# Tap products in an idle half of the result tile, a reciprocal-root chain one group later, and the last group's PSUM bank sets exchanged

## The chip, the core and the metric

The kernel runs on one core of a Trainium2 chip. The metric is the device time of one execution in microseconds (us). The engines are PE (TensorE, matrix products; PEld is its loading of the stationary operand), DVE (VectorE), ACT (ScalarE), POOL (GpSimd) and SP (SyncE); each runs its own instructions in order and waits on semaphores for the others. DMAs are issued from SP and from POOL.

## What is computed

The input x has the shape (8, 4224, 192). The first block is a causal depthwise convolution over the sequence with 7 taps; the 192 channels are in 8 heads of 24, and each head has one softmaxed set of taps. The second block normalizes each row of the result y (mean and variance over 192 channels), multiplies by a 192x768 matrix, applies relu, multiplies by a 768x192 matrix, and adds y.

```
w = softmax(weight, axis=-1)
out = np.einsum('hk,bskhg->bshg', w, x_unf)      # x_unf: 7 shifted copies of x
mu, var = mean(x), mean((x - mu)**2)             # x is out of the first block
xn = (x - mu) / np.sqrt(var + 1e-06) * g_ln
return x + np.maximum(xn @ w_ch1, 0.0) @ w_ch2
```

## The kernel before, in words

**Groups.** The rows are cut into 18 groups, 128 partitions with up to 16 rows (J) each. Group 0 has 6 rows per partition, group 1 has 8 (what is left over from all batches), groups 2 to 16 have 16, and group 17, the last, has 10. The centring and the gain are folded into the first matrix, and the reciprocal root of the variance (rstd) is applied to a row's result at the very end, since relu commutes with a positive factor. Groups 0 and 1 are multiplied plainly (`up`, `down`). From group 2 on, the two products are done by a Strassen-like scheme with seven products of quarter matrices in place of eight (`up_mixed` and `up_last`, then `down_fast`): sums of quarters of the weights and of y are formed ahead, and partial results are added from PSUM or by DMA.

**Order.** The schedule is by hand: each engine gets its instructions in the order in which the Python code emits them. While PE works on group g, ACT, DVE and POOL prepare group g+1. The convolution of a group is made of three pieces: ACT writes the first tap's product into y (`first_tap`, L366, instructions of L375), then the second tap's into a tile tb (`second_tap`, L385, instructions of L383), which is added to y by four accumulating DMAs that POOL issues (`add_in_parts`, L402, instructions of L406); DVE adds the other taps (`conv`, L414). For group 2 there is a `third_tap` as well: it writes into a tile third, is added to tb[2] by four DMAs, and DVE adds tb[2] to y with one large addition (L1051).

**Buffers.** tb has one buffer (pool tag "tb"), and so has "cs", from which third[2] comes. A second user of a tag waits until the first user's last reader is done. The result of the first product is held in `room`, one tile of 6·16·128 floats per partition (tag "ht"). Groups 0 and 1 use only its lower half or less; during the start the upper half holds constants and the raw weights. From group 2 on the whole tile is used. The results of groups 0 and 1 share one output tile ot (L931).

**PSUM.** There are eight banks. `take_set` (L123) hands out four at a time, the lower or the upper four; `take_bank` (L118) one at a time, in turn. The up stage of a group from 2 on takes two sets, called X and Y; then `down_fast` takes six banks, beginning with the one that stood first in the up stage. Its bank for column block c and product kind i is banks[2c + i] (L849 to L853): kind 0 uses the first, third and fifth, and kind 1 the others.

**The up stage of groups 2 to 16** (`up_mixed`, L601). There are two passes, `one` over a third of a quarter's columns and `two` over the rest, each of seven products that alternate between X and Y. Results that must be added to a quarter that is already in `room` go in one of two ways (`close`, L636): DVE adds them from PSUM (L640), or ACT copies them out (L634) and POOL issues an accumulating DMA (`add_by_dma`, L599). In pass `one` there are three such DMAs, whose sources lie in places of `room` that pass `two` writes later; so ACT's eviction of `two.c22` (L694) waits until the third has landed. Two calls of next(pending) stand between them: `pending` is the generator `root` (L447), 19 small POOL operations that compute rstd by Newton steps, nine before its first yield and ten after it. `act_scales` (L654) makes ACT scale two rows of the group before, one of them ahead of the eviction of c21 (L691), the second further on.

**The down stage** (`down_fast`, L839) has seven products on PE and sums on DVE (L899); ACT evicts (L862). Between the products it works through a list `work`, which up_mixed returns: relus, the scaling of the remaining rows of the group before (`scale`, L936, instructions of L938), the DMAs that add them to the output in DRAM (`add_to_out`, L940, issued by POOL at L949), and the first and second taps of group g+2.

**Around groups 0 to 2.** After down(0), the main loop calls `next(root(0, True))` (L1046), which emits all 19 POOL operations for groups 0 and 1 at once. In `down(1)` ACT evicts each row from PSUM with the scale applied (L812), and group 0's six rows are scaled and added to the output at its first step; parts of second_tap(3) stand between the evictions (L817). In group 1's step the main loop also emits DVE's convolution of group 2, its sums (L590 to L594, with POOL's L595 and L596), and the sums of weight quarters on POOL (L571). Group 1's output is added in group 2's work list (L721).

**The last group** (`up_last`, L726) has one pass with X and Y. Its last product goes into X, from where ACT evicts it with relu (L776). Then DVE lowers quarters (L834), and `down_fast` starts with the product of c11 (the quarter a[:, 0, 0]).

Of the kernel before, what the change touches and what calls it, by code (L numbers as in the profile page):

```python
# [7 lines left out]
F32 = mybir.dt.float32  # L8
# [8 lines left out]
def kernel(  # L17
# [29 lines left out]
    nc = tc.nc  # L47
# [337 lines left out]
    def second_tap(g, heads=(0, H)):  # L385

        if heads[0] == 0:
            tb[g] = bpool.tile([P, J, D], F32, tag="tb", name=f"tb{g}")
        tap_products(g, tb[g], 1, heads)
        if g > 2 and heads[1] == H:  # L390
            add_in_parts(g, y[g], tb[g])
# [3 lines left out]
    def third_tap(g, heads):  # L395
        if heads[0] == 0:
            third[g] = cpool.tile([P, J, D], F32, tag="cs", name=f"third{g}")
        tap_products(g, third[g], 2, heads)
        if heads[1] == H:
            add_in_parts(g, tb[g], third[g])  # L400
# [45 lines left out]

    def root(g, whole=False):  # L447
        both = [k for k in (g, g + 1) if k < NG and chain_of(k) == g]
# [25 lines left out]
        for step in range(3):  # L474
            nc.gpsimd.tensor_tensor(d, r, r, op=ALU.mult)  # L475
            nc.gpsimd.tensor_tensor(d, d, v, op=ALU.mult)  # L476
            if step == 0 and not whole:
                yield
            affine(d, d, -0.5, 1.5)
            nc.gpsimd.tensor_tensor(r, r, d, op=ALU.mult)  # L480
# [120 lines left out]
    def up_mixed(g, ahead, pending):  # L601
# [7 lines left out]
        s1, s2, s3, s4 = ysums[g]  # L609
        done = groups[g - 1][2] if fast[g - 1] else 0  # L610

# [42 lines left out]
        def act_scales(j1, j2):  # L654
            if done:
                scale(g - 1, j1, j2)

# [54 lines left out]
        def scale_one(j):  # L712
            scale(g - 1, j, j + 1)
            if j == 7:
                add_to_out(g - 1, 0, 8)
            elif j == done - 1:
                add_to_out(g - 1, 8, done)

        work = [lambda: one.relu(one.c22)]
        if g == 2:  # L720
            work += [lambda: add_to_out(1, 0, groups[1][2])] + [lambda: None] * 5  # L721
        work += [lambda j=j: scale_one(j) for j in range(2, done)]
# [3 lines left out]
    def up_last(g, ahead, pending):  # L726
# [22 lines left out]

        X, Y = take_set(), take_set()  # L750
        product(X, a11, b11, True, False)
# [46 lines left out]
    def down(g):  # L798
# [3 lines left out]
        for j in range(0, groups[g][2], 2):  # L802
            bank = take_bank()[:, 0 : 2 * D].rearrange("p (j d) -> p j d", d=D)
            for i in range(2):
                down_row(bank[:, i], lambda f: ht[g][:, f, j + i].rearrange("p q t -> p (q t)"))
            if g == 0:
                nc.scalar.copy(ot[:, j : j + 2, :], bank)
                if j:
                    third_tap(2, (0, 4) if j == 2 else (4, H))
                continue  # L810
            for i in range(j, j + 2):
                nc.scalar.mul(ot[:, i, :], bank[:, i - j], rstd[g][:, i : i + 1])  # L812
            if j == 0:
                scale(0, 0, groups[0][2])
                add_to_out(0, 0, groups[0][2])
            elif j < 6:
                second_tap(3, heads=(2, 5) if j == 2 else (5, H))  # L817

# [20 lines left out]
    def down_fast(g, work):  # L839
# [8 lines left out]
        parts = [free[:, 0:CH], free[:, CH : 2 * CH]]  # L848
        banks = [take_bank() for c in range(CH) for i in range(2)]  # L849

        def product(bank, left, right, to, first, behind=0):
# [83 lines left out]

    def scale(g, j1, j2):  # L936
        for j in range(j1, j2):
            nc.scalar.mul(ots[g][:, j, :], ots[g][:, j, :], rstd[g][:, j : j + 1])  # L938
# [77 lines left out]
    for g in range(NG):  # L1016
# [9 lines left out]
        if g == 0:  # L1026
# [18 lines left out]
            down(g)  # L1045
            next(root(0, True))  # L1046
            continue
        if g == 1:
# [13 lines left out]
            sums_of_quarters(w2sums[:, 1], b22, w2sums[:, 0])  # L1062
            sums_of_quarters(w2sums[:, 3], b21, w2sums[:, 1])
            continue
        if g + 2 < NG:
# [44 lines left out]
```

## Time and profile before

| | |
|---|---|
| runs shown | 961.76, 961.92, 963.83 us |
| median | 961.92 us |
| the profiled execution | 965.22 us |
| its span in the profile | 963.4 us |
| mean granted TensorE clock | 0.995 |
| POOL: DMAs that add to the output, L949 | 70 issues, 0.97 us each |
| ACT: scaling of rows, L938 | 230 instructions, 0.47 us each |
| median time from issue to landing: adds into room from room (512 KB) | 5.2 us |
| the same: adds of tap products to y (384 KB) | 8.9 us |

The span is that of the instructions that the profiler saw; the execution's own time lies 1.8 us above it. A profiled execution can differ from the runs without a profile; here it is 3.3 us above their median.

How to read it: a line of a timeline gives the start and the length in us, the engine, the line of the kernel, the operation, the tile written and the tile read, and how often; brackets at the end hold the idle time ahead of it and what ended that. A list of waits gives who waited for whom, with the total, the number of waits and the longest. A table of windows gives, for each stretch, its length, then the busy time of PE, PEld, DVE, ACT and POOL with their instructions, then the granted clock of TensorE, the share of the DMA engines and the rate in GB/s. "issue" as the releaser means that the profile shows nothing that was waited for; the landing of a DMA can be behind it.

### The profile page before, as it was taken

To read this page: it belongs to the slowest core of one execution; us is meant where nothing else is said; L and a number is where in the kernel's file an instruction comes from. 1 tells how busy PE (TensorE), PEld (TensorE's weight loads), DVE (VectorE), ACT (ScalarE), POOL (GpSimd) and SP (SyncE) were. 2 spreads that over 40 slices of the span, in tenths; PEclk is the share of its full clock that TensorE was granted. 3 is DMA by queue.
4 is the path that set the end of the run, shared out by engine and by line. 5 is a ranking of instruction groups with operands and counts; after the bars stand their busy time and mean duration, and the time that the engine had idled before them with its cause. 6 is when DMAs were issued, how large, how long until landed. Compare 5 with 4: busy or idle time off the path is not lost. (4 is left out here: it accounts for less than half of the span.)

```text
span 963.4 us, 38488 instructions
## 1 busy us (share of the span) xinstructions
PE 945.3 (98%) x17106; PEld 751.3 (78%) x17106; DVE 892.4 (93%) x1479; ACT 715.6 (74%) x1271; POOL 344.0 (36%) x463
## 2 busy tenths in 40 slices
PE   9999699999999999999999999999999999999998
PEld 7999558677785989778796967768596877869587
DVE  8995989999999999999999999999999999997885
ACT  6957566968788795968779696877879596767552
POOL 2077316141544218141452316241351425332140
PEclk9999999999999999999999999999999999999999
DMA  9387985897979787897978988797988888776641
GB/s 204 120 188 184 224 228 103 215 205 141 257 143 252 148 238 154 193 227 130 276 133 239 176 205 184 141 267 146 249 152 232 169 176 205 131 171 123 100 66 47
DMA packets 38347, 171.94 MB, mean 178 GB/s; under 512 B 4517, under 2 KB 5798, under 8 KB 32039
## 3 DMA queue, kind: packets, MB, share of 16 engines
q0 software_dynamic: 31488, 106.87, 60.3%
q1 hardware_dynamic: 6688, 62.61, 18.0%
q8 instruction: 134, 2.20, 0.9%
q14 instruction: 31, 0.25, 0.1%
q10 hardware_dynamic: 6, 0.00, 0.0%
HBM read 38.92 MB, written 50.92 MB: 93 GB/s over the span
## 5 line engine op out<-in xcount | busy, mean ns | idle before, releaser
L414 DVE SCALAR_TENSOR_TENSOR y<-xg,taps,y 128x384 f32<-128x384 f32 (+3 forms) x710 | 358.8, 580 | 13.9 <-issue 13.3
L856 PE MATMUL ps<-room,w2sums 128*32 128x256 f32 (+1 forms) x4464 | 243.1, 376 | 0.0
L634 ACT COPY room<-ps 128x512 f32<-128x512 f32 (+1 forms) x225 | 180.6, 845 | 65.6 <-PE ps L520 61.5
L520 PE MATMUL ps<-yt,w 32*128 32x256 f32 (+3 forms) x4092 | 226.3, 365 | 1.0 <-ACT ot L812 0.5
L520 PEld LDWEIGHTS ps<-yt,w 32*128 32x128 f32 x4092 | 203.2, 185 | 19.0 <-issue 6.8
L856 PEld LDWEIGHTS ps<-room,w2sums 128*32 128x32 f32 x4464 | 148.7, 110 | 88.7
L856 PE MATMUL ps<-room,w 128*32 128x256 f32 (+1 forms) x3456 | 194.6, 379 | 7.6 <-DVE room L640 5.7
L856 PEld LDWEIGHTS ps<-room,w 128*32 128x32 f32 x3456 | 115.2, 112 | 78.6 <-DVE room L640 10.8
L899 DVE TENSOR_TENSOR room<-room 128x1024 f32<-128x1024 f32 x135 | 154.6, 1218 | 19.1 <-PE ps L856 11.1
L520 PE MATMUL ps<-ysums,w1sums 32*128 32x256 f32 (+1 forms) x2304 | 132.2, 371 | 0.0
L520 PEld LDWEIGHTS ps<-ysums,w1sums 32*128 32x128 f32 x2304 | 121.3, 185 | 5.3 <-issue 0.2
L949 POOL DMA_DIRECT2D out_dram<-ot x70 | 60.4, 967 | 173.3 <-ACT ot L938 161.2
L862 ACT COPY cs<-ps 128x256 f32<-128x256 f32 (+1 forms) x192 | 70.9, 369 | 56.8 <-PE ps L856 56.4
L647 ACT ACTIVATE room<-room 128x1024 f32<-128x1024 f32 x90 | 94.8, 1063 | 4.1 <-DMA room<-parts_cs 4.1
L938 ACT ACTIVATE ot<-ot,r 128x192 f32<-128x192 f32 x230 | 97.2, 468 | 0.0
L406 POOL DMA_DIRECT2D y<-tb x59 | 52.9, 1426 | 116.1 <-ACT room L862 95.6
L520 PE MATMUL ps<-yt,w1sums 32*128 32x256 f32 (+1 forms) x1152 | 71.9, 372 | 2.8 <-ACT room L634 2.8
L375 ACT ACTIVATE y<-xg,taps 128x384 f32<-128x384 f32 (+3 forms) x141 | 72.9, 605 | 1.5 <-DMA xg<-in_x_dram 0.8
L383 ACT ACTIVATE tb<-xg,taps 128x384 f32<-128x384 f32 (+1 forms) x128 | 69.8, 625 | 5.5 <-DVE w1sums L568 5.5
L520 PE MATMUL ps<-ysums,w 32*128 32x256 f32 (+1 forms) x1152 | 71.2, 369 | 0.0
L445 DVE BATCH_NORM_STATS2 st<-y 128x6 f32<-128x192 f32 x264 | 70.2, 344 | 0.0
L862 ACT COPY room<-ps 128x256 f32<-128x256 f32 (+1 forms) x96 | 35.5, 371 | 44.0 <-PE ps L856 43.4
(125 smaller groups left out, 962.4 us busy)
## 6 DMA issues: line engine op xcount, KB each, us to landing
xg<-in_x_dram SPq DMA_DIRECT2D x14, 2112.0 KB, 15.9
out_dram<-ot POOLq DMA_DIRECT2D x61, 384.0 KB, 9.5
room<-room POOLq DMA_DIRECT2D x45, 512.0 KB, 5.2
y<-tb POOLq DMA_DIRECT2D x58, 384.0 KB, 8.9
out_dram<-y SPq DMA_DIRECT2D x14, 1536.0 KB, 9.5
room<-parts_cs POOLq DMA_DIRECT2D x30, 512.0 KB, 6.9
room<-parts_tb POOLq DMA_DIRECT2D x15, 1024.0 KB, 7.6
xg<-in_x_dram SPq DMA_DIRECT2D x1, 1848.0 KB
```

What stands on the lines that cost most here:

```text
L375: nc.scalar.mul(y[g][:, 0:n, cs], xg[g][:, 0:n, cs], taps[:, h, 0:1])
L383: nc.scalar.mul(dst[:, 0:n, cs], xg[g][:, k : k + n, cs], taps[:, h, k : k + 1])
L414: nc.vector.scalar_tensor_tensor(out=y[g][:, 0:n, cs], in0=t[:, k : k + n, cs], scalar=taps[:, h, k : k + 1], in1=y[g][:, 0:n, cs], op0=AL ...
L445: nc.vector.bn_stats(out=sums[g][:, j, :], in_=y[g][:, j, :])
L520: nc.tensor.matmul(banks[:, q, i * w + j1 * t : i * w + j2 * t], right[rows, c, P * i : P * i + P], left[rows, j1:j2, c, :], start=start, ...
L634: nc.scalar.activation(to, of, AF.Relu) if relu else nc.scalar.copy(to, of)
L647: nc.scalar.activation(c, c, AF.Relu)
L856: nc.tensor.matmul(dst[C * q : C * q + C, 0:w], right[:, f, C * c : C * c + C], left[:, f, q], start=(first and f == PAIR), stop=(f == PAI ...
L862: nc.scalar.copy(to[:, c], dst[:, 0:w].rearrange("p (j t) -> p j t", t=t))
L899: nc.vector.tensor_tensor(dst[:, f], left[:, f], right_of[:, f], op=op)
L938: nc.scalar.mul(ots[g][:, j, :], ots[g][:, j, :], rstd[g][:, j : j + 1])
L949: nc.gpsimd.dma_start(out=rows[:, d0:d1], in_=src[:, d0:d1], accum_op=ALU.add)
```

## The change

- tb[2] and third[2] are no longer tiles of their own: they are the two quarters of the upper half of `room`. The other groups' tb keep their tile.
- `root(0)` is no longer emitted after down(0). It becomes `pending` at the end of group 1's step, so that its two pieces are emitted in group 2's up stage, at the two calls of next(pending).
- `down(1)` evicts as `down(0)` does, two rows with one plain copy. The rows of groups 0 and 1, 14 together, are scaled in group 2 (two in the up stage, twelve in the work list of its down stage), and both groups are added to the output from that list. The second taps of group 3 are spread over the first three evictions of down(1), two or so heads after each.
- In the last group, X and Y are exchanged: X is the upper set. `down_fast` reorders its six banks there, so that kind 0 uses the first three and kind 1 the other three.

```
     def second_tap(g, heads=(0, H)):
-        if heads[0] == 0:
+        if heads[0] == 0 and g == 2:
+            tb[g] = room[:, NF * J * Q :][:, 0 : J * D].rearrange("p (j d) -> p j d", d=D)
+        elif heads[0] == 0:
             tb[g] = bpool.tile([P, J, D], F32, tag="tb", name=f"tb{g}")
...
     def third_tap(g, heads):
         if heads[0] == 0:
-            third[g] = cpool.tile([P, J, D], F32, tag="cs", name=f"third{g}")
+            third[g] = room[:, NF * J * Q + J * D :].rearrange("p (j d) -> p j d", d=D)
...
-    def root(g, whole=False):
+    def root(g):
...
-            if step == 0 and not whole:
+            if step == 0:
                 yield
...
     def up_mixed(g, ahead, pending):
-        done = groups[g - 1][2] if fast[g - 1] else 0
+        before = g - 1 if fast[g - 1] else 0
+        done = sum(groups[k][2] for k in range(before, g))
...
         def act_scales(j1, j2):
-            if done:
-                scale(g - 1, j1, j2)
+            scale(before, j1, j2)
...
         def scale_one(j):
-            scale(g - 1, j, j + 1)
-            if j == 7:
-                add_to_out(g - 1, 0, 8)
-            elif j == done - 1:
-                add_to_out(g - 1, 8, done)
+            scale(before, j, j + 1)
+            for k in range(before, g):
+                n = groups[k][2]
+                first, mid = (0 if k == before else groups[before][2]), min(8, n)
+                if j == first + mid - 1:
+                    add_to_out(k, 0, mid)
+                elif j == first + n - 1:
+                    add_to_out(k, mid, n)
...
-        if g == 2:
-            work += [lambda: add_to_out(1, 0, groups[1][2])] + [lambda: None] * 5
...
     def up_last(g, ahead, pending):
-        X, Y = take_set(), take_set()
+        Y, X = take_set(), take_set()
...
     def down(g):
-            if g == 0:
-                nc.scalar.copy(ot[:, j : j + 2, :], bank)
-                if j:
-                    third_tap(2, (0, 4) if j == 2 else (4, H))
-                continue
-            for i in range(j, j + 2):
-                nc.scalar.mul(ot[:, i, :], bank[:, i - j], rstd[g][:, i : i + 1])
-            if j == 0:
-                scale(0, 0, groups[0][2])
-                add_to_out(0, 0, groups[0][2])
-            elif j < 6:
-                second_tap(3, heads=(2, 5) if j == 2 else (5, H))
+            nc.scalar.copy(ot[:, j : j + 2, :], bank)
+            if g == 0 and j:
+                third_tap(2, (0, 4) if j == 2 else (4, H))
+            elif g == 1 and j < 6:
+                second_tap(3, heads=[(2, 4), (4, 6), (6, H)][j // 2])
...
     def down_fast(g, work):
         banks = [take_bank() for c in range(CH) for i in range(2)]
+        if g + 1 == NG:
+            banks = [banks[CH * i + c] for c in range(CH) for i in range(2)]
...
             down(g)
-            next(root(0, True))
             continue
...
             sums_of_quarters(w2sums[:, 3], b21, w2sums[:, 1])
+            pending = root(0)
             continue
```

## The prediction

> **What bounds the kernel.** I read the busy shares first. PE (TensorE) is busy 98% of the span and is full in nearly every slice; the fifth slice is the exception, the only place after the start where it drops visibly.
>
> ```profile
> PE 945.3 (98%) x17106; PEld 751.3 (78%) x17106; DVE 892.4 (93%) x1479; ACT 715.6 (74%) x1271; POOL 344.0 (36%) x463
> ...
> PE   9999699999999999999999999999999999999998
> ```
>
> So an edit pays only where PE waits, or where its clock falls. PE's own waits, second view, are few:
>
> ```profile
> PE ps L856 <- DVE room L640: 5.7, 2, 5.3
> PE ps L520 <- ACT room L634: 2.8, 3, 2.2
> ...
> PE ps L856 <- ACT room L776: 1.9, 1, 1.9
> PE ps L520 <- ACT ot L812: 0.5, 1, 0.5
> ```
>
> The timeline places them: 0.54 us at 82.9, 2.17 at 104.8 and 5.33 at 112.4, all in group 2 (the first full group), and 1.87 at 937.2 in the last group. Third view, PE in order of time (start, length, count, and in brackets the idle time before):
>
> ```profile
> 106.92 2.87 PE L520 MATMUL ps<-yt,w1sums 32*128 32x256 f32 x48 [2.17 <-ACT room L634]
> 109.62 2.77 PE L520 MATMUL ps<-yt,w 32*128 32x256 f32 x48
> 117.71 7.02 PE L856 MATMUL ps<-room,w 128*32 128x256 f32 x72 [5.33 <-DVE room L640]
> 124.56 7.94 PE L856 MATMUL ps<-room,w2sums 128*32 128x256 f32 x144
> 132.33 4.06 PE L856 MATMUL ps<-room,w 128*32 128x256 f32 x72
> ```
>
> 72 equal matmuls take 7.02 us after the long wait and 4.06 later: 2.96 lost to the clock. The windows (PE's granted clock is the figure ahead of the last two) agree, and show the same at the end:
>
> ```profile
> 116.00:118.00 2.00, 0.29 (x4) 0.20 (x8) 1.90 (x2) 0.00 (x0) 0.00 (x0) 0.72 1.17 151
> 118.00:120.00 2.00, 2.00 (x24) 0.94 (x20) 2.00 (x2) 0.00 (x0) 0.00 (x0) 0.50 0.89 96
> ...
> 941.00:943.00 2.00, 2.00 (x48) 1.98 (x44) 2.00 (x4) 0.40 (x2) 0.00 (x0) 0.52 0.04 8
> ```
>
> At the end, 72 narrow matmuls at 939.08 take 3.73 us, against 2.15 for the same form at 946.67: 1.58 lost.
>
> **Why PE waits in group 2.** DVE reaches the sum of L640 late because it sat idle for 12.30 us, waiting for the four DMAs that add group 3's tap products to y (L406). POOL issued those only behind other things:
>
> ```profile
> 80.19 2.86 POOL L595 TENSOR_TENSOR ysums<-yt 128x768 f32<-128x768 f32 x1 [2.82 <-DVE ysums L594]
> 83.00 1.80 POOL L949 DMA_DIRECT2D out_dram<-ot  x2
> 84.17 4.17 POOL L406 DMA_DIRECT2D y<-tb  x4
> 86.35 3.82 POOL L596 TENSOR_TENSOR yt<-yt,ysums 128x768 f32<-128x768 f32 x1
> ...
> 93.36 2.63 POOL L599 DMA_DIRECT2D room<-room  x3
> ```
>
> **Part 1, tap products into the free half.** ACT's second_tap(3) waited 5.51 us (69.1 to 74.66) for the old tb tile. With its own buffer free, ACT goes on at 69.1. down(1) is then paced by PE (16.05 us from 64.87), and with plain evictions ACT finishes group 3's products by about 78.5 instead of 82.6. That alone is worth little: the adds are behind L595 on POOL, which ends at 83.0, and L595 hangs on DVE, which this edit leaves alone. What moves the adds is that the two out_dram issues (1.80 us) no longer stand in front: 1.8 earlier, and 576 KB of accumulating traffic less ahead of them in DMAs that are full from 86 on. Before, the landing that freed DVE at 97.84 came 13.0 us after POOL got to the adds (84.8). Bounds for the new one: 96.0 (only the 1.8), and 92.6, if the last of the four, issued 2.7 after the first, lands in the 6.9 us that is the shortest landing of the same four adds a group later. With the median of all such adds, 8.9, it is 94.6; I take 94.5. DVE's 17.5 us from there to L640 (97.84 to 115.38) give 112.0. The 0.54 wait at 82.9 also goes, as a plain eviction frees the bank at once.
>
> **Part 2, the root a group later.** 19 small POOL operations leave 57 to 68.6, where POOL then idled (6.12 us before 74.73), so nothing is gained there. They land in group 2's queue, past L571, L595, the four adds, L596 and w2sums: nine between the first and second L599 add, ten between second and third. The price is seen in group 3: first L599 at 152.27, second at 156.34, third at 162.67, so 4.07 and 6.33. The first L599 moves 93.36 - 1.8 = 91.6, the third to 102.0 (before: about 95.1). Two waits follow.
> - ACT's first scale (L938, 0.47) stands ahead of the c21 eviction (1.87) and needs the root: 102.0 + 0.5 + 1.87 = 104.3. PE is ready for s1·b12 at 101.4 (101.99 less the 0.54): it waits 2.9, then works 2.75, to 107.1.
> - The c22 eviction needs the third add landed. A row of the chain of waits gives 5.82 us for that DMA (603.08, the same place in a later group); the median of all 45 is 5.2, the largest around group 2 is 13.5. I take 5.8, as nothing stands ahead of it any more: 107.8, evicted at 109.8. PE waits 2.7.
>
> Then a22·t2 ends at 112.5, L640 at 114.9, s4·b22 at 115.3. The down stage starts at 115.3, not 117.71: -2.4. DVE is off this path by 0.5 us; if its adds land at 96.0 it gives 115.8.
>
> The clock: this trace has a drop after waits of 5.33 and 1.87 us, and none after 2.17. Two waits of 2.9 and 2.7 with 2.75 of work between are inside that. Bounds: no loss, or the 2.96 of before; I take 1.7, near the 1.58 of the short wait (a drop during s1·b12 is hidden, since the third add ends that wait). Group 2: -2.4 - 2.96 + 1.7 = **-3.7**.
>
> The Trainium skill ("TensorE: Matmul & The Clock Gate", Part 1, What's actually happening) says that the clock halves after at least one idle window of about 3.4 us. The 1.87 us wait with 0.52 granted after it disagrees. By the rule neither new wait would cost clock, and group 2 would give -5.4.
>
> For the third add, the skill ("DMA: Bandwidth & Descriptors", Anatomy of one DMA) fits 2.0 us plus bytes over 436 GB/s, which I work out as an estimate of 3.2 us for 512 KB. The rows above, 5.2 and 5.8, disagree; by the rule that landing would be 2.6 us earlier, and DVE would then be the bound.
>
> **Part 3, scales and output adds later.** Fourteen scales (0.47 each) replace six and eight scaled evictions; twelve lie in group 2's down stage, where ACT is 15.6 of 24 us busy (120 to 144). Group 3 does the same beside 22.45 of 24 without a PE wait. Behind the ten output adds (0.87 each) on POOL are group 4's four adds. In group 3 the last scaled block is issued 12.1 us after the down stage starts; here the last eight then end near 117.0 + 12.1 + 7.0 = 136, and the four adds are ready 21.0 after the start (196.61 - 175.59), at 138. Cost nothing; with that cover gone, the next slack is some 5 us before DVE needs them at 155.
>
> **Part 4, last group.** X becomes the upper four banks. At the start, its first bank is the last that the stage before evicts (919.15 + 0.37): PE, ready at 919.02, waits 0.5. At the end the down stage's first three banks are Y's, last read by DVE's second close (934.30 + 2.15, plus 0.5 = 937.0), while PE ends at 937.7: the 1.87 wait goes. What is late next: the lowered sums (DVE, about 938 to 939), needed 2.15 later, at 939.9. DVE and stores at the end follow PE. Of the 1.7 lost to clock (1.58, and 0.15 in the next group of matmuls) I count 1.2, since a 2.17 wait cost nothing elsewhere. +0.5 - 1.87 - 1.2 = **-2.6**; bounds -1.3 and -3.1.
>
> **Sum:** -6.3. The profiled execution took 965.22 (span 963.4), so 958.9 there; the median of the runs, 961.92, is 3.3 lower, and I set the sum against it: **955.6**. A difference under 0.2%, 1.9 us, can't be told from no change here.
>
> **Rivals.**
> 1. *Waits exchanged* (0.22): the third add lands near 110 and the clock drops for the longer stretch. Down starts 2.2 later, at 117.5, and loses 2.96: group 2 gives nothing, and only the last group's -1.3 to -3.1 remain: 959.7. For it: POOL's root and ACT's scale are both ahead of what PE needs. Against: the DMAs ahead of the add have drained.
> 2. *The root holds the third add* (0.06), slower: it takes the 13.5 us seen around group 2, landing at 115.5. Down starts at 123.0 and loses 2.96 again: +5.3, less 2.6 at the end: 964.6. From a landing at 112.8 on nothing is left of the gain (group 2 then loses what the end gives); from 114.7 on the kernel is slower by 0.2%.
> 3. *Clock kept* (0.12): no drop in group 2: -5.4 - 3.1 = -8.5, 953.4.
> 4. Part 1 does nothing, since POOL holds the adds anyway: DVE gives at worst 115.8 and the total moves by 0.5; it is inside the forecast (0.60, 953.8 to 958.0).
>
> The range takes cases 1, 3 and the forecast: 952.8 to 960.6. Faster by over 0.2%: 0.60 + 0.12 + most of rival 1 (0.15) = 0.87; within: 0.07; slower: 0.06.
>
> **What would show it.** In the new profile: ACT's first tb product right behind the first taps of group 3; L406's adds at 83.0; DVE's idle time ending near 94.5; root operations between the L599 issues, the third at 102; PE waiting twice for ACT, near 101 and 107, and no longer for L640; in the last group a wait of 0.5 near the start, none for L776, and the clock at 1.00 to the end. Wrong if the third add lands after 110, if DVE still ends PE's wait, or if a wait appears in group 2's down stage.

## The result and the profile after

| | before | after |
|---|---|---|
| median of the runs | 961.98 us (6 runs, 961.71 to 963.83) | 958.47 us (6 runs, 956.92 to 959.96) |
| ratio, 95% interval | | 0.9958 [0.9944, 0.9972] |
| the profiled execution, its span | 965.22, 963.4 us | 958.28, 956.4 us |
| granted clock in it | 0.995 | 0.999 |

The change makes the kernel faster by 0.42%, some 3.5 to 4 us. The forecast was 6.3. The two profiled executions differ by 6.9, because that of before was 3.3 above its median and that of after is at its median. So the runs without a profile decide the size, and the traces show the places. When the two traces are compared by their clock times, 1.0 us must be added to those of after: down(0) starts 0.95 earlier there (36.27, against 37.22), ahead of the first instruction that the change touches, and down(1) too (63.92, against 64.87).

The busy shares and the list of PE's waits of the changed kernel (waiter, releaser, then the total, the number and the longest):

```profile
PE 940.8 (98%) x17106; PEld 742.7 (78%) x17106; DVE 892.3 (93%) x1479; ACT 716.6 (75%) x1275; POOL 340.6 (36%) x463
```

```profile
PE ps L522 <- ACT room L637: 4.2, 3, 2.3
...
PE ps L854 <- issue: 1.7, 3, 1.0
PE ps L854 <- DVE room L643: 1.2, 1, 1.2
...
PE ps L522 <- ACT cs L860: 0.5, 1, 0.5
```

The long wait for DVE has shrunk from 5.3 to 1.2, the waits for ACT have grown, the wait for the relu eviction has gone, and a releaser that was not on the list before has come: "issue". PE in order of time in group 2 (L522 is the up stage, L854 the down stage; before they were L520 and L856):

```profile
102.44 2.87 PE L522 MATMUL ps<-ysums,w 32*128 32x256 f32 x48 [2.31 <-ACT room L637]
106.80 2.87 PE L522 MATMUL ps<-yt,w1sums 32*128 32x256 f32 x48 [1.50 <-ACT room L637]
109.50 2.77 PE L522 MATMUL ps<-yt,w 32*128 32x256 f32 x48
113.51 4.09 PE L854 MATMUL ps<-room,w 128*32 128x256 f32 x72 [1.25 <-DVE room L643]
117.42 4.07 PE L854 MATMUL ps<-room,w2sums 128*32 128x256 f32 x72
121.79 4.31 PE L854 MATMUL ps<-room,w2sums 128*32 128x256 f32 x72 [0.30 <-issue]
```

Three waits of 2.31, 1.50 and 1.25 stand where there were 2.17 and 5.33, and the 72 matmuls behind the last one take 4.09, not 7.02. The windows of the same stretch, and of the last group, have the full clock (the figure ahead of the last two):

```profile
116.00:120.00 4.00, 4.00 (x80) 2.38 (x76) 4.00 (x8) 3.01 (x9) 1.73 (x2) 1.00 0.86 147
...
940.00:944.00 4.00, 3.98 (x148) 3.71 (x144) 1.13 (x4) 1.67 (x8) 0.00 (x0) 1.00 0.02 4
```

POOL in the same stretch: the adds of group 3's tap products (L408) come right behind L597, and the root's operations stand between the L601 adds.

```profile
79.21 2.85 POOL L597 TENSOR_TENSOR ysums<-yt 128x768 f32<-128x768 f32 x1 [2.76 <-DVE ysums L596]
82.00 3.54 POOL L408 DMA_DIRECT2D y<-tb  x4
...
90.56 0.87 POOL L601 DMA_DIRECT2D room<-room  x1
...
94.16 0.89 POOL L601 DMA_DIRECT2D room<-room  x1 [0.35 <-issue]
...
100.08 0.88 POOL L601 DMA_DIRECT2D room<-room  x1
```

DVE is released from its idle time at 93.63 (before 97.84), and works without a gap up to the close of c21 (L643), which PE's third wait is for:

```profile
93.63 14.91 DVE L416 SCALAR_TENSOR_TENSOR y<-xg,taps,y 128x384 f32<-128x384 f32 x28 [9.07 <-issue]
...
111.17 2.28 DVE L643 TENSOR_TENSOR room<-room,ps 128x2048 f32<-128x2048 f32 x1
```

ACT's two rows that PE's first two waits are for: the scale (L937) waits for the root, with the eviction of c21 queued behind it, and the eviction of c22 waits for the third add.

```profile
100.18 0.45 ACT L937 ACTIVATE ot<-ot,r 128x192 f32<-128x192 f32 x1 [3.25 <-POOL r L482]
...
104.88 1.86 ACT L637 COPY room<-ps 128x2048 f32<-128x2048 f32 x1 [1.54 <-DMA room<-room]
```

And PE in the last group:

```profile
913.08 5.17 PE L522 MATMUL ps<-yt,w 32*128 32x160 f32 x144 [0.49 <-ACT cs L860]
...
935.10 3.80 PE L854 MATMUL ps<-room,w2sums 128*32 128x128 f32 x131 [0.99 <-issue]
...
946.42 1.29 PE L854 MATMUL ps<-room,w 128*32 128x128 f32 x38 [0.41 <-issue]
947.64 4.17 PE L799 MATMUL ps<-w,kept 128*128 128x192 f32 x24
```

The 1.87 for the relu is gone. In its place stand 0.49 at the start and 0.99 and 0.41 in the down stage: 1.89.

### The profile page after: what moved, and what is told of

It reads as the page before. It is cut to its first block, busy times and chain, and to the rows that moved or that the text cites. A ratio compares the mean times of both kernels' runs of the same rounds, so it can differ in the third digit from the quotient of the medians.

```text
span 956.4 us, 38496 instructions
## 1 busy us (share of the span) xinstructions
PE 940.8 (98%) x17106; PEld 742.7 (78%) x17106; DVE 892.3 (93%) x1479; ACT 716.6 (75%) x1275; POOL 340.6 (36%) x463
## 5 line engine op out<-in xcount | busy, mean ns | idle before, releaser
L854 PE MATMUL ps<-room,w2sums 128*32 128x256 f32 (+1 forms) x4464 | 244.1, 376 | 1.3 <-issue 1.3
L522 PE MATMUL ps<-yt,w 32*128 32x256 f32 (+3 forms) x4092 | 226.3, 365 | 1.6 <-ACT room L512 1.0
L854 PEld LDWEIGHTS ps<-room,w2sums 128*32 128x32 f32 x4464 | 146.4, 110 | 93.1 <-issue 2.4
L522 PEld LDWEIGHTS ps<-yt,w 32*128 32x128 f32 x4092 | 203.2, 185 | 19.6 <-issue 7.2
L854 PE MATMUL ps<-room,w 128*32 128x256 f32 (+1 forms) x3456 | 191.0, 373 | 1.7 <-DVE room L643 1.2
L854 PEld LDWEIGHTS ps<-room,w 128*32 128x32 f32 x3456 | 111.6, 110 | 72.8 <-DVE room L643 6.4
L522 PE MATMUL ps<-ysums,w1sums 32*128 32x256 f32 (+1 forms) x2304 | 132.2, 371 | 0.0
L522 PEld LDWEIGHTS ps<-ysums,w1sums 32*128 32x128 f32 x2304 | 121.3, 185 | 5.3 <-issue 0.2
L860 ACT COPY cs<-ps 128x256 f32<-128x256 f32 (+1 forms) x192 | 70.6, 368 | 47.5 <-PE ps L854 47.1
L937 ACT ACTIVATE ot<-ot,r 128x192 f32<-128x192 f32 x238 | 100.8, 467 | 3.3 <-POOL r L482 3.3
L408 POOL DMA_DIRECT2D y<-tb x59 | 52.1, 1376 | 105.1 <-ACT room L860 98.2
L522 PE MATMUL ps<-yt,w1sums 32*128 32x256 f32 (+1 forms) x1152 | 71.6, 372 | 1.8 <-ACT room L637 1.8
L522 PE MATMUL ps<-ysums,w 32*128 32x256 f32 (+1 forms) x1152 | 71.1, 369 | 2.3 <-ACT room L637 2.3
L522 PEld LDWEIGHTS ps<-ysums,w 32*128 32x128 f32 x1152 | 62.6, 185 | 5.2 <-ACT room L637 2.7
L860 ACT COPY room<-ps 128x256 f32<-128x256 f32 (+1 forms) x96 | 35.6, 372 | 41.2 <-PE ps L854 40.6
```

What stands on the lines that cost most here:

```text
L408: nc.gpsimd.dma_start(out=ends[0], in_=ends[1], accum_op=ALU.add)
L522: nc.tensor.matmul(banks[:, q, i * w + j1 * t : i * w + j2 * t], right[rows, c, P * i : P * i + P], left[rows, j1:j2, c, :], start=start, ...
L854: nc.tensor.matmul(dst[C * q : C * q + C, 0:w], right[:, f, C * c : C * c + C], left[:, f, q], start=(first and f == PAIR), stop=(f == PAI ...
L860: nc.scalar.copy(to[:, c], dst[:, 0:w].rearrange("p (j t) -> p j t", t=t))
```

## The experiments

The theory drawn from the two profiles, called A: group 2 gives the whole gain, through the two output adds that no longer stand ahead of group 3's tap adds; the root costs nothing, as it only splits one wait; the exchange of banks in the last group gives nothing, as its wait comes back in other places. The rival B: each part gives about what the prediction gave it, and the difference from the forecast lies in the sizes.

The twelve kernels were timed in five rounds beside the kernel before, in three batches of four, in the order of the table; the changed kernel was timed apart from them, beside 961.98 for before. Across batches the ratios compare better than the medians. The time that the clock takes is worked out for each run as (1 - granted clock) x time; the clock of a run is known to 0.001, which is 1 us, so that only means over runs are used. In the profiled execution of before this gives 0.005 x 965 = 4.8, against 2.96 + 1.58 + 0.15 = 4.7 by the lengths of the matmuls.

| kernel | median us | ratio to before [95%] | lost to the clock, mean | mean time without it |
|---|---|---|---|---|
| before, beside each batch | 962.86, 962.25, 961.51 | | 4.2, 3.9, 4.2 | 958.3, 958.4, 957.7 |
| after | 958.47 | 0.9958 [0.9944, 0.9972] | 1.6 | 956.8 |
| before_again | 962.12 | 0.9999 [0.9988, 1.001] | 4.3 | 958.3 |
| last_only | 962.70 | 1.0003 [0.999, 1.0015] | 3.6 | 959.2 |
| all_but_last | 958.63 | 0.9963 [0.995, 0.9975] | 1.8 | 957.0 |
| root_early | 960.00 | 0.9977 [0.9965, 0.999] | 3.4 | 957.0 |
| taps_only | 963.39 | 1.0005 [0.9994, 1.0017] | 4.2 | 958.7 |
| outs_later | 959.63 | 0.9975 [0.9963, 0.9987] | 2.8 | 957.0 |
| last_no_adds | 955.70 | 0.9930 [0.9917, 0.9944] | 1.2 | 954.5 |
| adds_first | 959.02 | 0.9960 [0.9944, 0.9975] | 1.1 | 957.8 |
| best1 | 953.05 | 0.9905 [0.9887, 0.9922] | 0.8 | 952.1 |
| best2 | 960.91 | 0.9985 [0.9968, 1.0001] | 3.5 | 957.2 |
| best3 | 958.50 | 0.9981 [0.9962, 1.0001] | 3.8 | 956.1 |
| last_banks | 957.38 | 0.9953 [0.9937, 0.997] | 1.6 | 955.9 |

(One run of taps_only, at 1229.65, is left out of its two means.)

### before_again: the kernel before, profiled once more

> The kernel before, unchanged, to see how usual its profiled execution was. Theory A (the change gained what its waits say, and the clock loss of 2.96 and 1.7 us seen in that one execution is not in every run): the median is again near 962.0, and a second profile shows PE's three waits in group 2 (about 0.5, 2.2, 5.3) and the 1.9 us wait in the last group, but less time at a halved clock, with a span near 960. Theory B (the halved clock belongs to these waits): the second profile has a span near 963.4 with the halved clock in both places.

The same time, and the same clock after the same waits; PE in its last group, where 72 matmuls take 3.75 us, not the 2.17 they take at the full clock:

```profile
937.75 3.75 PE L856 MATMUL ps<-room,w 128*32 128x128 f32 x72 [1.87 <-ACT room L776]
```

So the two drops that the prediction counted belong to the kernel and not to one execution.

### last_only: the exchange in the last group alone

```
-        X, Y = take_set(), take_set()
+        Y, X = take_set(), take_set()
...
         banks = [take_bank() for c in range(CH) for i in range(2)]
+        if g + 1 == NG:
+            banks = [banks[CH * i + c] for c in range(CH) for i in range(2)]
```

> The kernel before with only the exchange of the bank sets in the last group. Theory A (the 1.87 us wait goes, but 0.5 us at the start and about 1.4 us of waits that the profile gives to issue come in its place, as in the profile after): 0 to -0.8 us against before. Theory B (the prediction's): -2.6 us, with -1.3 as the least.

It gives nothing: 1.0003 [0.999, 1.0015]. PE in the last group has no wait at the start of the down stage, and instead:

```profile
941.49 3.70 PE L858 MATMUL ps<-room,w2sums 128*32 128x128 f32 x128 [1.53 <-issue]
945.50 0.31 PE L858 MATMUL ps<-room,w2sums 128*32 128x128 f32 x3 [0.32 <-issue]
```

Together with the 0.49 of the up stage that is 2.34 for the 1.87 that went. The columns of the table say the same: 0.6 won from the clock, 0.9 lost elsewhere. In group 2, which this edit leaves alone, this execution shows a halved clock after a wait far shorter than the 5.33 of before (4.55 us for what takes 2.87):

```profile
107.76 4.55 PE L520 MATMUL ps<-yt,w1sums 32*128 32x256 f32 x48 [2.45 <-ACT room L634]
```

### all_but_last: the whole change without that exchange

```
-        Y, X = take_set(), take_set()
+        X, Y = take_set(), take_set()
...
-        if g + 1 == NG:
-            banks = [banks[CH * i + c] for c in range(CH) for i in range(2)]
```

> The change without its part in the last group (bank sets as before). Theory A (nearly all of the gain is in group 2): -2.8 to -3.5 us against before, about the same as the whole change. Theory B (the prediction's split): the last group's part is worth 2.6 of it, so this gives some -1 us against before, if the whole gives -3.5.

958.63 against 958.47 for the whole change: the exchange gives nothing on top of the rest either. The two traces compare best by the stretch from the end of the last up product to the start of L799, which holds the whole down stage with what is waited for ahead of it: 931.59 to 947.64 in after, 932.08 to 948.13 here, 16.05 us in both. What differs from before, where it is 17.43, is the clock: the same 1.87 us wait leaves it full in this execution. One pair of traces says little, as the stretch varies: in the seven traces with the exchange and all its DMAs it is 15.91 to 17.04, to which the 0.49 at the start comes (17.0 on average), and in the five without it 17.42 to 17.43 four times and 16.05 here (17.15 on average).

```profile
933.95 2.17 PE L852 MATMUL ps<-room,w 128*32 128x128 f32 x72 [1.87 <-ACT room L779]
935.94 4.11 PE L852 MATMUL ps<-room,w2sums 128*32 128x128 f32 x144
```

### root_early: the changed kernel with the root after down(0)

```
             down(g)
+            for step in root(0):
+                pass
             continue
...
-            pending = root(0)
```

> The whole change, but all 19 root operations for groups 0 and 1 are emitted after down(0) again, where POOL idles; the scales stay in group 2. Theory A (DVE's sum in group 2 ends PE's wait either way, so the later root costs nothing): PE's two waits for ACT (2.31 and 1.50) vanish, and one wait for DVE's sum of about 5 us stands in their place; the down stage of group 2 starts within 0.3 us of the change's 113.5, and the time is the same, or up to 3 us longer if the longer single wait halves the clock. Theory B (the prediction's: the root on POOL sets when the third add lands and so when PE goes on): the down stage starts 1 to 3 us earlier and the time falls by as much.

The waits for ACT nearly vanish (0.41 is left), and the down stage starts at 113.16, near that of after (113.51; the start-up lay 0.7 us ahead here): the wait for DVE's L643 has taken all of it.

```profile
102.38 2.87 PE L522 MATMUL ps<-yt,w1sums 32*128 32x256 f32 x48 [0.41 <-ACT room L637]
105.08 2.77 PE L522 MATMUL ps<-yt,w 32*128 32x256 f32 x48
113.16 6.77 PE L854 MATMUL ps<-room,w 128*32 128x256 f32 x72 [5.32 <-DVE room L643]
```

So the later root costs nothing. In the trace of after it turns one wait of 5.3 into three of at most 2.3, and after the one wait the clock is halved (6.77 for what takes 4.09). In the means the change loses 1.6 to the clock and this kernel 3.4, at the same time without it (956.8 and 957.0). The split doesn't keep the clock in every execution: see last_banks below.

### taps_only: only the tiles of group 2's tap products, in the kernel before

```
+        if heads[0] == 0 and g == 2:
+            tb[g] = room[:, NF * J * Q :][:, 0 : J * D].rearrange("p (j d) -> p j d", d=D)
...
-            third[g] = cpool.tile([P, J, D], F32, tag="cs", name=f"third{g}")
+            third[g] = room[:, NF * J * Q + J * D :].rearrange("p (j d) -> p j d", d=D)
```

> The kernel before with only the tap products of group 2 in the free half of the result tile; roots, scales, output adds and the last group as before. Theory A (POOL's queue sets when group 3's products are added, not ACT): ACT's wait of 5.5 us goes, but the two output adds and L595 still stand ahead of the four adds on POOL; DVE still starts its part for group 3 about 97.8 us into the span (give or take the 1 us by which starts differ), and the time is that of before, 0 to -0.6 us. Theory B (the freed tile is what makes the adds early): -2 us or more.

1.0005 [0.9994, 1.0017]. ACT no longer waits for the tile, but POOL's order is the old one, L951 (the output adds) ahead of L408, and DVE starts at 97.75:

```profile
80.33 2.85 POOL L597 TENSOR_TENSOR ysums<-yt 128x768 f32<-128x768 f32 x1 [2.82 <-DVE ysums L596]
83.12 1.79 POOL L951 DMA_DIRECT2D out_dram<-ot  x2
84.29 4.16 POOL L408 DMA_DIRECT2D y<-tb  x4
...
97.75 14.91 DVE L416 SCALAR_TENSOR_TENSOR y<-xg,taps,y 128x384 f32<-128x384 f32 x28 [12.08 <-issue]
```

### outs_later: root early, and the old tiles; only the output adds and scales are later

It is root_early with the edit of taps_only undone:

```
-        if heads[0] == 0 and g == 2:
-            tb[g] = room[:, NF * J * Q :][:, 0 : J * D].rearrange("p (j d) -> p j d", d=D)
...
-            third[g] = room[:, NF * J * Q + J * D :].rearrange("p (j d) -> p j d", d=D)
+            third[g] = cpool.tile([P, J, D], F32, tag="cs", name=f"third{g}")
```

> The change with the root emitted early (as in the run with the root early) and, besides, the tap products back in tiles of their own. What is left is the later scaling and the later output adds of groups 0 and 1, and the last group's exchange. Theory A: the later output adds alone move group 3's four adds forward, so the time is that of the run with the root early, 960.0 within 0.5. Theory B (the free half is needed for it): it goes back toward before, 961.5 or more.

959.63, against 960.00 for root_early: the free half is not needed for the gain. POOL gets to the adds at 82.28 and DVE is released at 94.12:

```profile
94.12 14.91 DVE L414 SCALAR_TENSOR_TENSOR y<-xg,taps,y 128x384 f32<-128x384 f32 x28 [9.30 <-issue]
```

Of the change's three parts around group 2, then, the later scales and output adds move the landing without the other two. What the later root does to the clock is known only on top of them, from root_early; no run has it without them.

### last_no_adds: what the issue waits in the last group come from

The four DMAs that add the last but one group's rows to the output (1.57 MB) are left out, so their rows lack that part.

```
-            add_to_out(g - 1, j1, j1 + HJ)
```

> The whole change, but the last group doesn't add the group before to the output: these four DMAs (1.57 MB) are left out, so that part of the output lacks a term. Theory A (the waits of 0.99 and 0.41 us that the profile gives to issue in the last down stage are PE's instructions, whose transfers are late behind this traffic): these waits vanish or fall below 0.3 us together, and the span falls by about 1.4 us. Theory B (they are a semaphore wait that the profile doesn't show, or a limit of PE's own): they stay, within 0.3 us, and the time is unchanged within 0.5.

The issue waits are gone, and the products stand back to back:

```profile
931.07 2.17 PE L853 MATMUL ps<-room,w 128*32 128x128 f32 x72
933.06 4.11 PE L853 MATMUL ps<-room,w2sums 128*32 128x128 f32 x144
936.99 2.15 PE L853 MATMUL ps<-room,w 128*32 128x128 f32 x72
```

The stretch from the last up product to L799 is 13.82 us here (931.15 to 944.97), against 16.05 in after and in all_but_last, and 17.43 in before, of which 1.87 is the wait and 1.73 the clock: 13.83. So 13.8 is what the work itself takes, and the DMAs' traffic, which keeps 0.73 of the DMA engines busy between 931 and 934 in after and 0.02 here, puts 2.2 us into it once PE does not wait for the relu (1.4 of it in the two issue waits). The first of these waits begins at 934.11 in after, when DVE's lowered sums (done at 932.52) and ACT's eviction with relu (933.42) lie behind. That PE waits for its own instructions, which come by DMA as well (the profile's queue "q8 instruction", 134 packets with 2.20 MB), behind that traffic, would explain that nothing in the program is named as releaser; no run tried it by itself, so this is an inference.

### adds_first: POOL issues the tap adds ahead of its sums of y

```
+            down(g)
             fourth_sum = sums_of_y(2, nc.gpsimd)
             nc.vector.tensor_tensor(w12, w12, w11, op=ALU.subtract)
             moments(2)
-            down(g)
```

> The whole change, and besides, POOL issues group 3's four adds ahead of its two operations on sums of y (L595 and L596 of before): the sums, the moments and the subtraction on w are emitted behind down(1). Theory A (DVE's wait for these adds is what ends PE's last wait in group 2): DVE starts about 4 us earlier, near 89.6, PE's wait for its sum (1.25 us) goes, the two waits for ACT (2.3 and 1.5) stay, and the time falls by 1 to 1.5 us against the change. Theory B (the root sets the pace there): no change within 0.5 us.

The wait for DVE went, as expected of A, and the gain did not come: 959.02. Two waits for ACT stay, and an issue wait takes the place of the third. Group 2's up stage starts 2.4 us later here than in after (82.58, against 80.22), so that only the brackets are compared:

```profile
105.25 2.87 PE L522 MATMUL ps<-ysums,w 32*128 32x256 f32 x48 [2.76 <-ACT room L637]
109.63 2.87 PE L522 MATMUL ps<-yt,w1sums 32*128 32x256 f32 x48 [1.51 <-ACT room L637]
...
115.02 4.09 PE L854 MATMUL ps<-room,w 128*32 128x256 f32 x72
...
124.40 3.88 PE L854 MATMUL ps<-room,w2sums 128*32 128x256 f32 x64 [1.40 <-issue]
```

Counted from the start of the up stage, the down stage starts 0.85 us earlier than in after (32.44 us behind it, not 33.29), and the issue wait is 1.10 longer (1.40, not 0.30). This one has a cause in the program. The product behind it adds to the banks from which ACT copies c22, and that copy (L860) stands in ACT's queue behind a relu that waits for the add of parts_tb to land:

```profile
122.99 1.06 ACT L650 ACTIVATE room<-room 128x1024 f32<-128x1024 f32 x1 [2.12 <-DMA room<-parts_tb]
123.95 0.36 ACT L860 COPY cs<-ps 128x256 f32<-128x256 f32 x1
```

The copy ends at 124.31, and PE goes on 0.09 later. In after, all_but_last and last_banks, too, PE ends its issue wait in group 2 about 0.1 us after this copy. By the code and these times, group 2's issue waits are the landing of that DMA (issued at 111.98 here), and an earlier start of the down stage runs into it.

### best1: root early and adds first together

```
             down(g)
+            for step in root(0):
+                pass
             continue
...
+            down(g)
             fourth_sum = sums_of_y(2, nc.gpsimd)
             nc.vector.tensor_tensor(w12, w12, w11, op=ALU.subtract)
             moments(2)
-            down(g)
...
-            pending = root(0)
```

> The changed kernel with two edits that were each run alone: the root of the first two groups right after down(0) again, and POOL issuing group 3's four tap adds ahead of its sums of y of group 2. Theory A (each shift of a wait in group 2 is answered by the next one in line, and what ends last is DVE's chain to L643 or the landing of ACT's relu sums): PE's waits for ACT (2.31 and 1.50) shrink below 1, DVE reaches L643 near 109 to 110, the down stage starts at 111 to 112, and an issue wait of 1 to 2 us in the down stage takes back most of it; clock full or nearly so; ratio to the kernel before 0.993 to 0.996. Theory B (the three waits are additive, each microsecond taken off is kept): the down stage starts near 110 with no issue wait of over 0.4, ratio 0.991 to 0.993.

0.9905 [0.9887, 0.9922]: 8.5 us less than before by the medians, and about 5 less than after. It is the fastest kernel of this study that does the whole work. Theory A, which had held so far that every wait taken away is answered by another, fails here, and B's figures are met (the ratio even lies below its 0.991): the down stage starts at 110.47 without an issue wait behind it in group 2: the add of parts_tb, issued at 106.42, has landed when ACT comes to its relu at 115.88. (In the last group the issue waits stay, 1.42 and 0.33.)

```profile
106.44 2.96 PE L522 MATMUL ps<-yt,w 32*128 32x256 f32 x48
110.47 4.09 PE L854 MATMUL ps<-room,w 128*32 128x256 f32 x72 [1.07 <-DVE room L643]
114.38 7.95 PE L854 MATMUL ps<-room,w2sums 128*32 128x256 f32 x144
```

The row of DVE says why: it starts earlier. (The list names an eviction as the releaser; the last of the four adds of L408, issued from 79.7 to 81.4, landed 8.8 us after its issue or less, so at just about 90, and is the likelier one.)

```profile
90.59 14.91 DVE L416 SCALAR_TENSOR_TENSOR y<-xg,taps,y 128x384 f32<-128x384 f32 x28 [4.73 <-ACT room L637]
```

Two chains of nearly the same length lead to the down stage: POOL's root and the third add, by ACT; and the tap adds, by DVE. root_early shortened the first and adds_first the second, and each alone left the other. Both together give what neither gave. (In this execution group 2's up stage started 1.5 us later than in that of after, and the down stage still starts 3.0 earlier.) In the last column 952.1 stands against 956.8, and the clock gives another 0.8: most of the difference is waits.

### best2: DVE's close of c21 ahead of eleven convolution instructions

```
-        conv(g + 1, 2, 5)
-        conv(g + 1, 5, 6, heads=(0, H // 2))
+        if g == 2:
+            conv(g + 1, 2, 4)
+            conv(g + 1, 4, 5, heads=(0, H // 2))
...
         p.close(p.c21, X)
...
+        if g == 2:
+            conv(g + 1, 4, 5, heads=(H // 2, H))
+            conv(g + 1, 5, 6)
```

> As the run with root and adds early, and for group 2 alone DVE's close of c21 (L643) is moved ahead of 11 of the convolution's instructions (about 5.9 us at 0.53 each), so that DVE no longer ends PE's wait. Theory A: PE's wait for L643 is gone and the one for ACT's eviction (the third add into room) remains, 1 to 2 us; group 3's convolution ends no later for PE; ratio 0.990 to 0.994, unless issue waits of 1.5 in the down stage return. Theory B: no wait over 1 us remains in group 2; the down stage starts near 108 to 109; ratio 0.989 to 0.991. A third possibility: group 3's up stage starts late because DVE's convolution and sums are pushed back by the split; then a PE wait at about 135 to 140 shows for DVE and the ratio is 0.996 or above.

Slower than best1 by 7.9 us by the medians; the profiled execution, 957.69, was its fastest, so that the trace explains 3.6 of it (spans of 955.8 and 952.2). The down stage starts at 107.43 without a wait, as B expected, but the instructions that were put behind the close now stand ahead of DVE's sums for the down stage (L906), and PE stops there, with the clock halved behind it (9.66 for what takes 7.95):

```profile
127.30 9.66 PE L863 MATMUL ps<-room,w2sums 128*32 128x256 f32 x144 [3.93 <-DVE room L906]
```

It is the third possibility of the expectation, earlier than it put it. The 1.07 us that PE still waits for DVE in best1 can't be had by this order: in group 2 DVE has no slack behind the close.

### best3: best2 without the exchange in the last group

Its edit is that of all_but_last, made in best2.

> As the run before it, with the last group's sets and banks as in the kernel before. Theory A (the exchange at the end is worth nothing, since its waits move and add up to the same): within 0.15% of the run before it; in the last group one wait of 1.87 for the relu eviction and no issue waits. Theory B (the exchange is worth something once group 2 runs undisturbed): slower than the run before it by 1.3 to 2.6 us.

0.9981 [0.9962, 1.0001] against best2's 0.9985 [0.9968, 1.0001]: no difference that can be told, so the exchange has shown no gain in three pairs (with intervals of some 1.5 us to either side, a gain below that is not excluded). The wait of 1.87 is back, and the clock is halved after it (3.17 for 72 matmuls).

### last_banks: the sets as before, and other banks for kind 0

```
-        Y, X = take_set(), take_set()
+        X, Y = take_set(), take_set()
...
-            banks = [banks[CH * i + c] for c in range(CH) for i in range(2)]
+            eight = banks + [take_bank() for i in range(2)]
+            banks = [eight[4 * (1 - i) + c] for c in range(CH) for i in range(2)]
+            turn[0] -= 1
```

> The changed kernel, but in the last group X and Y stay as before, and the down stage's six banks are taken so that kind 0 gets three of the set that DVE closed earlier. Theory A (what limits the last down stage is the arrival of the instructions behind the output adds, so that any wait removed ahead of it comes back as issue waits): the 0.49 at the start of the up stage is gone, the 1.87 for the relu is gone, and issue waits of together 1.3 to 2.0 appear; time within 0.1% of the changed kernel. Theory B (the 0.49 is a cost of its own): 0.5 us faster than the changed kernel, issue waits 1.4 as there.

Both waits are gone, that of 0.49 too, and issue waits of 1.47, 0.32 and 0.41 have come, 2.2 together, a little above A's 1.3 to 2.0; the stretch up to L799 is 17.09 us, 1.04 more than in after, for 0.49 saved at its start. 0.9953 [0.9937, 0.997] beside the 0.9958 of after tells no difference. A is favoured by the trace; the times alone would not tell it from B.

Its group 2 is that of the changed kernel, and this execution shows it otherwise than the trace of after does: the first wait is 3.31 and the clock is halved behind it (1.7 us lost by 48 matmuls), the second is gone.

```profile
102.53 4.56 PE L522 MATMUL ps<-ysums,w 32*128 32x256 f32 x48 [3.31 <-ACT room L637]
...
933.65 3.70 PE L856 MATMUL ps<-room,w2sums 128*32 128x128 f32 x128 [1.47 <-issue]
```

## Why the prediction was right in direction and too large

**Part 1, the tap products.** Right, in each number that the trace shows: the free tile alone is worth nothing (taps_only), the output adds are what held the tap adds. With the 1.0 of the start-up added to the times of after, POOL gets to the adds at 83.0 (83.0 forecast), they release DVE at 94.6 (94.5), and DVE reaches the close of c21 17.5 us later, at 112.2 (112.0). root_early and outs_later give this alone: 0.9977 [0.9965, 0.999] and 0.9975 [0.9963, 0.9987].

**Part 2, the root a group later.** The two waits for ACT are there, 2.31 and 1.50 for 2.9 and 2.7. The second is shorter because the third add landed in 4.8 us, not in the 5.8 that I took, and was issued 0.9 earlier (101.1 with the start-up, 102.0 forecast). The step "DVE is off this path by 0.5 us" failed for the same reason: with both waits shorter DVE ended the third, of 1.25. The prediction had named that as a sign against itself, and a wait in group 2's down stage as another, which came too (0.30). What followed is small, as the down stage starts at 114.5 with the start-up, against 115.3. The estimate of 3.2 us for that landing, worked out from the Trainium skill ("DMA: Bandwidth & Descriptors", Anatomy of one DMA), lies further from the 4.8 than the rows of 5.2 and 5.8. The clock: 1.7 lost was forecast, and in the trace of after nothing was; in that of last_banks, with the same group 2, 1.7 was. Over the runs of all_but_last 1.8 are lost in the whole kernel, against 4.2 in before.

**Part 4, the last group.** The step that failed is "What is late next: the lowered sums (DVE, about 938 to 939), needed 2.15 later". They were in time. Late next was something that the trace of before shows at no place near there: PE's issue waits, beside the drain of the output adds, which 1.87 us of waiting for the relu had covered. The start costs 0.49 (0.5 forecast). The term of -2.6 measured about nothing: 1.0003 alone, and 958.47 beside 958.63 on top of the rest. Its part for the clock, -1.2, is not there either: the exchange brings the loss from 4.2 to 3.6 in last_only, and from 1.8 to 1.6 on top of the rest. Why all_but_last, which keeps the 1.87 us wait, loses so little stays open (the granted clock of its runs goes from 0.996 to 1.000).

**The sum.** Over the runs the change takes 2.6 from the clock (4.2 to 1.6); the forecast had 2.96 - 1.7 + 1.2 = 2.5. It takes 1.5 from the waits (958.3 to 956.8); the forecast had 2.4 + 1.37 = 3.8. By parts, the 2.3 too much is the last group's -2.6: without the exchange (all_but_last) the change takes 3.7 by the means (962.5 to 958.8), and 3.7 is what was forecast for group 2. That this meets is luck, for its two terms were off and cancel: the waits gave 1.3 for 2.4, and the clock, over the whole kernel, gave 2.4 for 2.96 - 1.7 = 1.3.

By the traces the waits of group 2 fell by 2.7 (0.54 + 2.17 + 5.33 before; 2.31 + 1.50 + 1.25 + 0.30 after), by the means of all_but_last only by 1.3. As a trace shows one execution and the profiled ones of before are longer than its median, it stays open where the other 1.4 are in the runs without a profile.

**The rivals.** None of them is what happened. The third add landed well before rival 1's 110; rival 2's 13.5 us landing did not come (in before it is that of the add of parts_tb, 1024 KB; the longest of the three adds from room, of 512 KB each, took 10.4 there); the clock was kept in the trace of after, as rival 3 had it, but the rest of its -8.5 was not. Rival 4 is half right: the tile alone does nothing, but the output adds do.

**What stays open** is when the clock drops. In the traces of groups from 2 on, single waits of 3.0 us and more were followed by the halved clock each time (nine waits, 3.02 to 5.38). Of the shorter ones, 2.45 was (last_only), and 2.76, 2.31, 2.17 and 1.96 were not; 1.87 was in four traces and not in the fifth. That fifth is all_but_last, the only one of them with no drop in group 2. The Trainium skill ("TensorE: Matmul & The Clock Gate", Part 1, What's actually happening) speaks of at least one idle window of about 3.4 us, and of a window that runs freely, so that the moment of a change depends on where in it the matmuls begin. That the same wait goes both ways agrees with the second; the drops after 1.87, 2.45 and 3.02 do not agree with the first.

## What to carry to other kernels

When a wait is taken away, write down what is late next on every engine that feeds the waiting one, and test the shortened chains together: here two edits that each gave nothing on top of the change gave about 5 us as a pair. An instruction's place in the queue of an engine that mostly idles (POOL's output adds) can matter more than the work it does, and a DMA issued there can cost the ones behind it as well: here DVE was released 11.6 us after POOL got to the tap adds, not 13.0, once the output adds came later. One wait of 5.3 us cost more than about the same time in three pieces, as the clock was halved after it. Where a list gives "issue" as the releaser, look at what the waiting product shares with other engines: in group 2 a landing stood behind it.

## What the runs showed of the hardware that was not expected

- PE waits without a releaser in the program while output adds drain: 0.99 and 0.41 us in the last group of after, up to 1.55 in adds_first, none there when those four DMAs are left out. The matmuls are narrowest there (144 of 128 columns in 4.11 us, 28.5 ns each; those of 256 columns take 55), so instructions are used up fastest; that this is the cause is not shown. The issue waits of group 2 are of another kind (adds_first).
- Three waits of 2.31, 1.50 and 1.25 us within 13.4 us leave the clock at 1.00 in after, while a single one of 5.3 halves it for 5 to 6 us (2.7 and 3.0 us lost by the 72 matmuls behind it, in root_early and in before).
- Small POOL operations on 128x14 take 0.21 us while DVE idles and 0.45 beside its convolution (the root's two pieces in after, from 92.1 on and from 95.5 on).
- The start, up to down(1), differs by up to 3.7 us between executions of kernels that are equal there (down(1) starts at 63.13 in last_banks, 63.92 in after and 66.78 in adds_first), which is as much as the effects studied here.
